# Attention ahead of routed experts, one core: other places for the pieces of the routing tables

## The chip, the core and the metric

One core of a Trainium2 chip runs the whole program. The metric is the device time of one execution in microseconds (us). The engines are TensorE (PE), VectorE (DVE), ScalarE (ACT), GpSimd (POOL) and SyncE (SP), which here only issues transfers.

## The reference, cut

```python
# q, k, v: (8, 8, 1152, 64); w_gate: (512, 8); w1: (8, 512, 1024); w2: (8, 1024, 512)
q_pool = q.reshape(B, H, S // 2, 2, D).mean(axis=3)
scores = q_pool @ k.T / sqrt(D)
attn = softmax(scores)                       # 1152 keys, row maximum subtracted
x = (attn @ v) -> (4608, 512)
logits = x @ w_gate                          # 8 experts, 576 tokens each at most
# tokens go to experts in the order of all logits, the largest first
for e in range(8):
    out[mask_e] = relu(x[mask_e] @ w1[e]) @ w2[e]
```

## The kernel before, in words

The 64 heads are worked on in 32 pairs of two heads. A pair has 18 steps, one for each head and block of 128 keys (`step`). In a step TensorE forms the scores of 576 pooled queries (L751), ScalarE writes their exponentials P in float32 (L754), and a remainder PM is formed, which is P less its upper sixteen bits, in float16 (L758). Of the eighteen remainders of a pair sixteen run on GpSimd and two, in all pairs but the first and the last, on VectorE (steps 4 and 12, `AT["pd"]`). Five steps later TensorE multiplies both parts with the values (L768).

While a pair is in these steps the next one is prepared: QS, KD and VD are loaded; one load of QS, which adds the second of two queries to the first, is issued by GpSimd (L486), once a pair. VectorE forms the low parts QL (L591) and KL in two halves (L610), and those of the values (L645). For an upper bound of the scores TensorE multiplies KH with the queries and VectorE takes maxima from two PSUM banks (L671, L680), gathers them (L703) and, after a transpose on TensorE (L723), writes AU (L724), which a transfer puts into QB. TensorE's next product into bank mb waits for AU.

The second half of the program routes the tokens and runs the experts. It needs constants (a triangle, counting rows, a diagonal, `slots`, `same16` and others), which `routing_tables` makes (L299 to L345): counts with iota first, then fifteen pieces on GpSimd and one on VectorE. They are handed out one to a pair, from the fourth pair on: `table` (L956) raises `od.base` by one with each piece. All of them write the key "tables", so in the planned order each one stands behind the one ahead of it, whichever engine has it.

The order of all work in the attention is set by `Cycle.plan`: an item's key is a number from the table TAU (by its tag, in a cycle of 25) plus 25 times its pair; items are taken by the least key once all that they need has been taken, and each engine's instructions are written in that order. The tag of GpSimd's pieces is "tab", that of VectorE's "tad", that of the remainders "pm". A piece that is planned does not wait for the one ahead on another engine at run time, unless it reads what that wrote.

Of the kernel before, what the change touches and what calls it, by code (L numbers as in the profile page):

```python
# [22 lines left out]
OP = mybir.AluOpType  # L23
# [129 lines left out]
class Cycle(Order):  # L153
# [11 lines left out]
    def plan(self):  # L165
# [45 lines left out]
       12.1143, 0.0557, 20.0132, 22.5039, 25.3261, 28.3165], "ql": [-38.1313], "rc": [9.2364, -9.47], "sc":  # L211
       [-36.4174], "scv": [-30.065], "spr": [-21.9235, -31.1405, -21.9627, -26.5265, -22.5479, -164.2155, -315.3032,
       -74.6622, -15.1485, -17.1123, -19.956, -16.4269], "store": [-95.7261], "sx": [16.3692, 22.2312, 0.8466,
       -61.2066, -78.1894], "tab": [-69.9737], "tad": [-127.8336], "tap": [-44.6145, -41.1498, -47.4908, -31.2065],
       "vh": [-26.7285, -47.8828], "vl": [-23.1603, -21.3115], "vs": [-148.6017, -208.4574], "vsh": [-168.3274],
       "wsq": [12.8365], "x": [-94.3595, -7.6786]}
TAU0 = {"abk": [-60.377, -62.9993], "abs": [-96.8953, -53.0217], "aug": [-7.39949, -0.804], "augt": [-7.399491,
# [58 lines left out]
def routing_tables(nc, pool, ident, jp, scratch, do):  # L276

    J = NBLK
    G = nc.gpsimd

    def one(shape, dt, name):
        return pool.tile(shape, dt, name=name)

    C = dict(ident=ident, before=one([128, 128], BF, "before"), upto=one([128, 128], BF, "upto"),
             ones=one([128, 128], BF, "mones"), e8=one([128, J, E], BF, "e8"), pcol=one([128, 1], F32, "pcol"),
             nib=one([128, 5, 16], F32, "nib"), diag=one([128, 64], F16, "diag"), same16=one([128, 128], F16, "same16"),
             slots=one([128, 640], F16, "slots"), slot1=one([128, 5], F32, "slot1"), jval=one([128, J], F32, "jval"),
             zero=one([128, J], F32, "zero"), TAB=one([128, 2, J + 2], F16, "TAB"), pcol2=one([128, 2], F32, "pcol2"),
             U=one([128, J], F32, "U"), asg=one([128, J], BF, "asg"), CAPS=one([128, E], F32, "CAPS"),
             KC=one([128, 2 * E + 6 + 3 * J], F32, "KC"), ru=one([128, J], BF, "ru"), W=one([128, 40, E], BF, "W"))  # L290
    it = {}
    at = 0
    for name, n in (("e8", J * E), ("p", 1), ("16", 16), ("d", 64), ("m", 128), ("s", 640), ("s1", 5), ("p2", 2)):
        it[name] = scratch[:, at:at + n]
        at += n
    it8 = it["e8"].rearrange("p (j e) -> p j e", e=E)

    def count(dur, ap, pattern, base, step):
        do("POOL", dur, lambda: nc.gpsimd.iota(ap, pattern=pattern, base=base, channel_multiplier=step))  # L299

    count(680, it8, [[0, J], [-1, E]], E, 0)
    count(80, it["p"], [[0, 1]], 0, 1)
    count(80, it["p2"], [[1, 2]], 0, 2)
    count(100, it["16"], [[1, 16]], 1, 0)
    count(210, it["d"], [[-16, 8], [0, 8]], 0, 1)
    count(240, it["m"], [[-1, 128]], 128, 1)
    count(1150, it["s"], [[1, 640]], 0, 0)
    count(90, it["s1"], [[128, 5]], 1, 1)

    def state():  # L310
        nc.gpsimd.memset(C["ones"], 1.0)
        nc.gpsimd.memset(C["zero"], 0.0)
        nc.gpsimd.memset(C["U"], 1.0)
        nc.gpsimd.memset(C["asg"], 0.0)
        nc.gpsimd.memset(C["CAPS"], float(CAP))

        KC = C["KC"]
        nc.gpsimd.memset(KC, 0.0)
        for q in range(5):
            nc.gpsimd.memset(KC[:, 2 * E + q:2 * E + q + 1], 16.0 ** q / 2)  # L320
        nc.gpsimd.memset(KC[:, 2 * E + 6:2 * E + 6 + J], float(CAP))
    do("POOL", 210, state)

    k1 = scratch.bitcast(F32)[:, at:at + 64]
    pieces = [
        (250, lambda: G.tensor_scalar(C["before"], jp, 0.0, None, op0=OP.is_gt)),
        (250, lambda: G.tensor_scalar(C["upto"], jp, 0.0, None, op0=OP.is_ge)),
        (600, lambda: G.tensor_copy(C["e8"], it8)),
        (120, lambda: (G.tensor_copy(C["pcol"], it["p"]), G.tensor_copy(C["pcol2"], it["p2"])))]
    for t in range(4):  # L330
        pieces.append((130, lambda t=t: (G.tensor_scalar(C["nib"][:, t], it["16"], float(16 ** t), None, op0=OP.mult),
                                         G.memset(C["nib"][:, t, 15:16], 3e9))))
    pieces += [
        (70, lambda: G.tensor_scalar(C["nib"][:, 4], it["16"], -1.0, None, op0=OP.add)),
        (250, lambda: (G.tensor_scalar(k1, it["d"], 0.0, None, op0=OP.is_ge),
                       G.tensor_scalar(C["diag"], it["d"], 16.0, None, op0=OP.is_lt))),
        (120, lambda: G.tensor_tensor(C["diag"], C["diag"], k1, op=OP.mult)),
        (1000, lambda: (nc.vector.tensor_scalar(it["m"], it["m"], 15, None, op0=OP.bitwise_and),
                       nc.vector.tensor_scalar(C["same16"], it["m"], 0.0, None, op0=OP.is_equal))),
        (1200, lambda: G.tensor_copy(C["slots"], it["s"])),  # L340
        (160, lambda: (G.tensor_copy(C["slot1"], it["s1"]),
                       G.tensor_scalar(C["jval"], it["s"][:, :J], 128.0, None, op0=OP.mult))),
        (120, lambda: [G.tensor_copy(C["TAB"][:, z, J + 1:J + 2], it["p"]) for z in range(2)]),
        (130, lambda: (G.tensor_copy(C["KC"][:, :E], C["e8"][:, 0]),
                       G.tensor_copy(C["KC"][:, 2 * E + 5:2 * E + 6], C["pcol"])))]  # L345
    for dur, fn in pieces:
        do("DVE" if dur == 1000 else "piece", dur, fn)
    return C


def attention(ctx, tc, top, kt, qt, v, wg, w1, x_dram, L, npair=NPAIR):
# [604 lines left out]
    def table(eng, dur, fn):  # L956
        pools.append(eng == "POOL")
        od.base = max(4, od.base + 1) if eng != "POOL" else 2 + sum(pools) // 4
        od.add(NSTEP * (od.base + 1), "DVE" if eng == "DVE" else "POOL", dur, fn, w=["tables"], lock=True,
               tag={"DVE": "tad", "POOL": "tap", "piece": "tab"}[eng])  # L960
    C = routing_tables(nc, top, ident, jp, scratch, table)
    early += best_early(C)
    if npair > H * NE:
# [687 lines left out]
```

## Time and profile before

| | us |
|---|---|
| three timed runs | 1263.82, 1265.13, 1270.05 |
| their median | 1265.13 |
| the profiled execution | 1275.09 |
| its span, from the first instruction to the last | 1273.3 |
| attention, to the gate's last product, about | 800 |
| granted clock of TensorE, mean | 0.98 |

All views are of the one profiled execution. A row of an engine's order of time has the start, the length, the engine, the line, the operation, what it writes and reads, how many were merged, and in brackets how long the engine had stood idle and what ended that. The length counts from the start of an instruction on its engine, so it holds time in which the instruction is held up there.

### The profile page before, as it was taken

What the parts mean: (1) busy time and instruction counts of PE and PEld (TensorE: products, weight loads), DVE (VectorE), ACT (ScalarE), POOL (GpSimd) and SP (SyncE); (2) the same over time, 40 slices, a digit from 0 to 9 for tenths busy, and PEclk for the clock granted to TensorE, in tenths of its full rate; (3) what the DMA queues carried; (4) which work ended last, traced back from release to release, by engine and by line L of the source; (5) the groups of instructions that cost most, each with busy time, mean ns of one, the idle gap of its engine ahead of it and who ended that gap; (6) DMA issues with size and microseconds to landing.
All of it is one profiled execution on the core that took longest, in us unless ns stands there. A gap on an engine that the chain in (4) does not pass through costs nothing.

```text
span 1273.3 us, 38899 instructions
## 1 busy us (share of the span) xinstructions
PE 1202.7 (94%) x15470; PEld 865.0 (68%) x15470; DVE 1034.3 (81%) x2743; ACT 974.6 (77%) x1719; POOL 905.9 (71%) x879
## 2 busy tenths in 40 slices
PE   7899899898999999999999999789899899999998
PEld 2567677776777777877777778565657466565563
DVE  5889899898999999999999995788878788884520
ACT  6779789797899999999999986076765676767751
POOL 5779799697889988888898897055756474665641
PEclk7999999898999999999999999999999999999999
DMA  6676677566667768677776731043254454537401
GB/s 184 159 187 171 155 174 189 142 163 164 170 162 196 178 163 203 169 171 192 174 187 162 183 91 37 20 170 112 97 195 125 133 172 135 170 124 230 119 30 38
DMA packets 131218, 190.83 MB, mean 150 GB/s; under 512 B 50268, under 2 KB 86108, under 8 KB 128732
## 3 DMA queue, kind: packets, MB, share of 16 engines
q1 hardware_dynamic: 117948, 126.75, 37.9%
q0 software_dynamic: 12944, 61.58, 17.0%
q8 instruction: 121, 1.98, 0.7%
q14 instruction: 61, 0.50, 0.1%
q10 hardware_dynamic: 144, 0.02, 0.0%
HBM read 116.41 MB, written 18.87 MB: 106 GB/s over the span
## 4 chain that ended last, share of the span: by engine, by line
PE 69%; DVE 17%; ACT 4%; issue 3%; DMA 3%; SPq 1%; POOL 1%; another core or an unknown queue 1%; POOLq 0%; ACTq 0%; DVEq 0%
PE sc L751 19%; PE av L768 16%; PE ph L1536 9%; PE po L1566 8%; PE mb L668 5%; PE ma L668 4%; DVE MX L671 2%; DVE KL L610 1%; PE av L803 1%; DMA XG<-XB 1%; DVE PM L758 1%; DVE GE L1163 1%; DVE HX L1545 1%; DMA BD<-QH 1%; PE av L815 1%
## 5 line engine op out<-in xcount | busy, mean ns | idle before, releaser
L758 POOL TENSOR_TENSOR PM<-P 128x576 f16<-128x576 f32 x508 | 618.3, 1277 | 117.2 <-ACT P L754 65.2
L754 ACT ACTIVATE P<-sc,EX 128x576 f32<-128x576 f32 x576 | 412.7, 738 | 97.2 <-PE sc L751 84.2
L768 PEld LDWEIGHTS <-P 128*128 128x128 bf16 x5760 | 297.2, 98 | 31.3 <-issue 2.6
L768 PE MATMUL av<-V,P 128*128 128x65 f16 (+1 forms) x5760 | 305.3, 193 | 0.0
L768 PE MATMUL av<-V,PM 128*128 128x65 f16 x2880 | 296.4, 195 | 0.0
L768 PEld LDWEIGHTS <-PM 128*128 128x128 f16 x2880 | 265.7, 97 | 0.0
L751 PE MATMUL sc<-QA,KA 128*128 128x288 f16 x1152 | 236.7, 287 | 1.6 <-ACT P L754 1.3
L751 PE MATMUL sc<-QB,KB 65*128 65x288 f16 (+1 forms) x1152 | 237.9, 287 | 0.0
L671 DVE TENSOR_REDUCE MX<-mb 128x1 f32<-128x512 f32 x279 | 190.9, 684 | 32.3 <-PE mb L668 27.3
L671 DVE TENSOR_REDUCE MX<-ma 128x1 f32<-128x512 f32 x279 | 191.0, 685 | 13.3 <-PE ma L668 10.1
L751 PEld LDWEIGHTS <-KA 128*128 128x128 f16 x1152 | 106.9, 97 | 86.0 <-issue 34.9
L1566 PE MATMUL po<-W2H,HX 128*128 128x512 f16 x512 | 156.9, 381 | 0.3 <-ACT OT L1568 0.3
L1536 PE MATMUL ph<-XH,W1H 128*128 128x320 f16 (+1 forms) x512 | 146.3, 286 | 0.7 <-DVE WE L1514 0.3
L1536 PE MATMUL ph<-XL,W1H 128*128 128x320 f16 (+1 forms) x512 | 146.2, 286 | 0.8 <-DVE XL L1395 0.3
L1536 PE MATMUL ph<-XH,W1L 128*128 128x320 f16 (+1 forms) x512 | 145.9, 286 | 0.9 <-issue 0.9
L751 PEld LDWEIGHTS <-KB 65*128 65x128 f16 (+1 forms) x1152 | 113.3, 98 | 30.4
L1566 PEld LDWEIGHTS <-HX 128*128 128x128 f16 x768 | 71.6, 98 | 86.4 <-issue 9.6
L1588 POOL DMA_INDIRECT out_dram<-OT,idx x40 | 39.1, 979 | 118.9 <-ACT OT L1568 99.7
L668 PE MATMUL mb<-KH,BD 128*128 128x512 f16 x279 | 107.3, 384 | 13.6 <-DVE AU L724 11.3
L1536 PEld LDWEIGHTS <-W1H 128*128 128x128 f16 x1024 | 97.5, 98 | 33.2 <-issue 7.7
L668 PE MATMUL ma<-KH,BD 128*128 128x512 f16 x279 | 106.8, 383 | 5.9 <-DMA BD<-QH 2.4
L1489 POOL TENSOR_TENSOR W2L<-W,W2H 128x512 f16<-128x512 f32 x64 | 73.3, 1158 | 40.8 <-ACT W L1487 33.6
(308 smaller groups left out, 2169.7 us busy)
## 6 DMA issues: line engine op xcount, KB each, us to landing
KD<-in_kt_dram SPq DMA_DIRECT2D x64, 288.0 KB
VD<-in_v_dram SPq DMA_DIRECT2D x32, 576.0 KB
WB<-in_w_dram SPq DMA_DIRECT2D x32, 512.0 KB
QA<-QH SPq DMA_DIRECT2D x128, 72.0 KB
KA<-KH SPq DMA_DIRECT2D x64, 144.0 KB
KA<-KL SPq DMA_DIRECT2D x64, 144.0 KB
KB<-KH SPq DMA_DIRECT2D x64, 144.0 KB
x_dram<-X SPq DMA_DIRECT2D x16, 576.0 KB
```

The lines of the kernel that those rows point to most:

```text
L610: fn=lambda h=h: nc.vector.scalar_tensor_tensor(KL[n % 2][:, h], KD[n % 2][:, h], KS, KH[i][:, h], op0=OP.mult, op1=OP.subtract),
L668: od.add(t, "PE", 214, lambda: nc.tensor.matmul(m, BD[i][:, j, :], KH[i][:, 512 * c:512 * c + 512], start=True, stop=True), r=bd + [("KH", ...
L671: od.add(t, "DVE", 597, lambda: nc.vector.tensor_reduce(MX[i][:, j, c:c + 1], m, axis=AX.X, op=OP.max), r=[mk], w=[("MX", i, j, c)], tag=" ...
L751: nc.tensor.matmul(c[:, t, :288], a[i][:rows, s, ks], b[i][:rows, s, 288 * t:288 * t + 288], start=first, stop=not first)
L754: od.add(g + 0.1, "ACT", 624, lambda: nc.scalar.activation(p.rearrange("p (t q) -> p t q", t=2), c[:, :, :288], AF.Exp, scale=EX[n % 3][:, ...
L758: od.add(g + 0.2, en, dur, lock=1, fn=lambda: eng.tensor_tensor(pm, p, hi, op=OP.subtract), r=[("P32", g % NP)], w=[("PM", g % NM)], tag="pm")
L768: nc.tensor.matmul(out, w[:, qs], v, start=kb == 0 and j == 0 and y == 0, stop=kb == NKB - 1 and y == 2, skip_group_check=True)
L803: nc.tensor.transpose(m[:, 128 * z:128 * z + 128], X[u][:, 3 * q + z], ident)
L1489: od.add(tt, "POOL", 1230, lambda o=lo[p], a=raw[p], h=hi[p]: nc.gpsimd.tensor_tensor(o, a, h, op=OP.subtract), r=[key, hk, sk], w=[(nm + ...
L1536: nc.tensor.matmul(p, a[:, d, fs], b[:, d, qs], start=z == 0, stop=z == 11)
L1566: nc.tensor.matmul(o, a[:, z, q0:q0 + 128], b[:, z], start=z == 0 and y == 0, stop=z == 7 and y == 2)
L1588: st = nc.gpsimd.indirect_dma_start(out=out, out_offset=bass.IndirectOffsetOnAxis(ap=idx[i][:n, c:c + 1], axis=0), in_=OT[ob][:n], in_offs ...
```

## The change

The key of GpSimd's pieces goes from -69.9737 to -60.4, later by 9.57 in the cycle of 25. VectorE's piece, two operations that were one item, becomes two items. Each item raises the pair by one, so the four pieces behind it (slots, slot1 with jval, TAB, KC) go one pair later as well. No instruction is added or taken away.

```diff
--- before.py
+++ after.py
@@ -211,7 +211,7 @@
        12.1143, 0.0557, 20.0132, 22.5039, 25.3261, 28.3165], "ql": [-38.1313], "rc": [9.2364, -9.47], "sc":
        [-36.4174], "scv": [-30.065], "spr": [-21.9235, -31.1405, -21.9627, -26.5265, -22.5479, -164.2155, -315.3032,
        -74.6622, -15.1485, -17.1123, -19.956, -16.4269], "store": [-95.7261], "sx": [16.3692, 22.2312, 0.8466,
-       -61.2066, -78.1894], "tab": [-69.9737], "tad": [-127.8336], "tap": [-44.6145, -41.1498, -47.4908, -31.2065],
+       -61.2066, -78.1894], "tab": [-60.4], "tad": [-127.8336], "tap": [-44.6145, -41.1498, -47.4908, -31.2065],
        "vh": [-26.7285, -47.8828], "vl": [-23.1603, -21.3115], "vs": [-148.6017, -208.4574], "vsh": [-168.3274],
        "wsq": [12.8365], "x": [-94.3595, -7.6786]}
 TAU0 = {"abk": [-60.377, -62.9993], "abs": [-96.8953, -53.0217], "aug": [-7.39949, -0.804], "augt": [-7.399491,
@@ -335,8 +335,8 @@
         (250, lambda: (G.tensor_scalar(k1, it["d"], 0.0, None, op0=OP.is_ge),
                        G.tensor_scalar(C["diag"], it["d"], 16.0, None, op0=OP.is_lt))),
         (120, lambda: G.tensor_tensor(C["diag"], C["diag"], k1, op=OP.mult)),
-        (1000, lambda: (nc.vector.tensor_scalar(it["m"], it["m"], 15, None, op0=OP.bitwise_and),
-                       nc.vector.tensor_scalar(C["same16"], it["m"], 0.0, None, op0=OP.is_equal))),
+        (1000, lambda: nc.vector.tensor_scalar(it["m"], it["m"], 15, None, op0=OP.bitwise_and)),
+        (1000, lambda: nc.vector.tensor_scalar(C["same16"], it["m"], 0.0, None, op0=OP.is_equal)),
         (1200, lambda: G.tensor_copy(C["slots"], it["s"])),
         (160, lambda: (G.tensor_copy(C["slot1"], it["s1"]),
                        G.tensor_scalar(C["jval"], it["s"][:, :J], 128.0, None, op0=OP.mult))),
```

GpSimd, from the remainder ahead of the piece upto (L327) to behind the next load of QS, before:

```order
L758 TENSOR_TENSOR PM_153<-P_143 128x576
L758 TENSOR_TENSOR PM_156<-P_146 128x576
L327 TENSOR_SCALAR upto<-jp 128x128
L758 TENSOR_TENSOR PM_155<-P_145 128x576
L758 TENSOR_TENSOR PM_157<-P_147 128x576
L758 TENSOR_TENSOR PM_150<-P_140 128x576
L758 TENSOR_TENSOR PM_159<-P_149 128x576
L758 TENSOR_TENSOR PM_152<-P_142 128x576
L758 TENSOR_TENSOR PM_151<-P_141 128x576
L758 TENSOR_TENSOR PM_153<-P_143 128x576
L486 DMA QS_124<-in_qt_dram 128x576
```

The same place in the changed kernel:

```order
L758 TENSOR_TENSOR PM_159<-P_149 128x576
L758 TENSOR_TENSOR PM_152<-P_142 128x576
L758 TENSOR_TENSOR PM_151<-P_141 128x576
L327 TENSOR_SCALAR upto<-jp 128x128
L758 TENSOR_TENSOR PM_153<-P_143 128x576
L486 DMA QS_124<-in_qt_dram 128x576
L758 TENSOR_TENSOR PM_154<-P_144 128x576
```

The piece has moved past six remainders and stands behind all but one of those ahead of the load L486. The other pieces move alike, the first (L326) past two remainders only.

VectorE, both places of its piece (- before, + the changed kernel):

```order
@@ -555,6 +555,4 @@
 L645 SCALAR_TENSOR_TENSOR V_104<-VD_123,SC_114,V_104 128x9x64
 L671 TENSOR_REDUCE MX_139<-mb 128x1
-L338 TENSOR_SCALAR scratch<-scratch 128x128
-L339 TENSOR_SCALAR same_182<-scratch 128x128
 L680 TENSOR_REDUCE MX_139<-ma 128x4
 L671 TENSOR_REDUCE MX_139<-mb 128x1
@@ -577,4 +575,6 @@
 L680 TENSOR_REDUCE MX_139<-mb 128x4
 L671 TENSOR_REDUCE MX_139<-ma 128x1
+L338 TENSOR_SCALAR scratch<-scratch 128x128
+L339 TENSOR_SCALAR same_182<-scratch 128x128
 L591 SCALAR_TENSOR_TENSOR QL_91<-QS_124,SC_115,QH_89 128x576
 L610 SCALAR_TENSOR_TENSOR KL_87<-KD_119,SC_115,KH_85 128x576
```

The two operations (L338, L339) leave the maxima of the value stage and stand directly ahead of QL (L591) and KL (L610).

## Rows read from the trace of the kernel before

**Rows 1.** The page's part 1: busy us, share of the span, instructions.

```profile
PE 1202.7 (94%) x15470; PEld 865.0 (68%) x15470; DVE 1034.3 (81%) x2743; ACT 974.6 (77%) x1719; POOL 905.9 (71%) x879
```

**Rows 2.** Busy times by stretch; PEclk is the granted clock; cut at L724.

```profile
core 0: us, PE busy (x) PEld busy (x) DVE busy (x) ACT busy (x) POOL busy (x), PEclk, DMA share, GB/s
518.56:702.47 183.91, 183.41 (x3050) 145.54 (x3051) 169.58 (x336) 168.91 (x293) 159.07 (x137) 1.00 0.73 179
107.86:158.93 51.07, 47.31 (x762) 37.45 (x761) 46.49 (x85) 42.01 (x74) 40.46 (x37) 0.97 0.62 163
204.98:257.59 52.61, 48.89 (x764) 38.27 (x761) 46.53 (x84) 42.40 (x74) 40.31 (x39) 0.94 0.63 157
281.15:332.98 51.83, 47.90 (x757) 37.28 (x755) 46.60 (x84) 42.37 (x73) 40.63 (x38) 0.93 0.63 159
136.00:140.00 4.00, 4.00 (x54) 3.26 (x51) 2.06 (x4) 3.08 (x5) 1.84 (x2) 0.57 0.54 137
332.98:357.30 24.32, 23.13 (x373) 18.21 (x373) 22.37 (x45) 21.04 (x38) 20.12 (x19) 1.00 0.73 183
```

**Rows 3.** VectorE in order of time, stalled pair: start us, us, what.

```profile
123.89 1.32 DVE L758 TENSOR_TENSOR PM<-P 128x576 f16<-128x576 f32 x1
...
127.79 1.70 DVE L758 TENSOR_TENSOR PM<-P 128x576 f16<-128x576 f32 x1
...
130.43 3.29 DVE L610 SCALAR_TENSOR_TENSOR KL<-KD,SC,KH 128x576 f16<-128x576 f32 x1
...
134.52 0.33 DVE L724 TENSOR_SCALAR AU<-mb,EX 9x128 f16<-9x128 f32 x1
```

**Rows 4.** GpSimd in order of time, the same stretch.

```profile
123.46 2.76 POOL L758 TENSOR_TENSOR PM<-P 128x576 f16<-128x576 f32 x2
127.73 1.15 POOL L758 TENSOR_TENSOR PM<-P 128x576 f16<-128x576 f32 x1 [1.51 <-issue]
128.82 0.88 POOL L486 DMA_DIRECT2D QS<-in_qt_dram  x1
129.47 3.62 POOL L758 TENSOR_TENSOR PM<-P 128x576 f16<-128x576 f32 x3
```

**Rows 5.** TensorE in order of time: two waits, in brackets.

```profile
134.90 0.38 PE L668 MATMUL mb<-KH,BD 128*128 128x512 f16 x1 [3.35 <-DVE AU L724]
343.35 0.38 PE L668 MATMUL ma<-KH,BD 128*128 128x512 f16 x1 [1.08 <-DVE MX L680]
```

**Rows 6.** VectorE in order of time, undisturbed pair.

```profile
375.62 0.81 DVE L591 SCALAR_TENSOR_TENSOR QL<-QS,SC,QH 128x576 f16<-128x576 f32 x1
376.34 0.81 DVE L610 SCALAR_TENSOR_TENSOR KL<-KD,SC,KH 128x576 f16<-128x576 f32 x1
377.07 0.75 DVE L758 TENSOR_TENSOR PM<-P 128x576 f16<-128x576 f32 x1
...
378.75 0.81 DVE L610 SCALAR_TENSOR_TENSOR KL<-KD,SC,KH 128x576 f16<-128x576 f32 x1
```

**Rows 7.** GpSimd in order of time, the same stretch.

```profile
374.29 1.21 POOL L758 TENSOR_TENSOR PM<-P 128x576 f16<-128x576 f32 x1 [0.41 <-ACT P L754]
377.56 1.26 POOL L758 TENSOR_TENSOR PM<-P 128x576 f16<-128x576 f32 x1 [2.06 <-issue]
378.77 0.87 POOL L486 DMA_DIRECT2D QS<-in_qt_dram  x1
```

**Rows 8.** VectorE and GpSimd in order of time, third stall.

```profile
302.18 0.90 POOL L486 DMA_DIRECT2D QS<-in_qt_dram  x1
...
302.49 4.59 DVE L610 SCALAR_TENSOR_TENSOR KL<-KD,SC,KH 128x576 f16<-128x576 f32 x1 [0.25 <-issue]
```

**Rows 9.** GpSimd in order of time: two pieces of the tables.

```profile
118.52 0.54 POOL L327 TENSOR_SCALAR upto<-jp 128x128 bf16<-128x128 int32 x1
...
391.03 0.71 POOL L340 CAST slots<-scratch 128x640 f16<-128x640 int32 x1
```

**Rows 10.** VectorE in order of time: its piece of the tables.

```profile
341.03 0.56 DVE L338 TENSOR_SCALAR scratch<-scratch 128x128 int32<-128x128 int32 x1
341.63 1.07 DVE L339 TENSOR_SCALAR same<-scratch 128x128 f16<-128x128 int32 x1
```

## The prediction

> **What bounds the kernel now.** I read the page first, for the busiest engine [rows 1]: TensorE is busy 94% of the span and nothing else is near it. Then the busy times by stretch, cut where VectorE writes AU (L724), which it does once in each pair of heads [rows 2]. Eight pairs from 518.56 to 702.47 take 183.91 us, 22.99 a pair, with TensorE busy 183.41 of it at a granted clock of 1.00: there TensorE is the bound and GpSimd's lateness costs nothing. The pieces of the tables all lie earlier. There, three stretches of two pairs each take 51.07, 52.61 and 51.83 us where 2 x 22.99 = 45.98 would do, at a mean clock of 0.97, 0.94 and 0.93. They are 5.09, 6.63 and 5.85 us too long, 17.57 together. That is the sum which this change can touch.
>
> Next, VectorE's order of time inside the first such stretch [rows 3]. The second half of KL (L610) starts at 130.43 and takes 3.29 us; one unhindered takes 0.81, as the second L610 row of the undisturbed pair shows [rows 6]. AU stands behind it and comes at 134.52, and TensorE has then waited 3.35 us for it [rows 5]; behind that wait, from 136 to 140, the granted clock is 0.57 [rows 2], near the lower of its two levels (1.2 of 2.4 GHz), and most of the remaining loss lies there. GpSimd's order of time [rows 4] shows what holds KL: a load of QS is issued at 128.82, and behind it three remainders run without a gap from 129.47 to 133.09. KL ends 0.6 us after the last of them.
>
> In an undisturbed pair [rows 6, 7] KL starts at 378.75, together with GpSimd's issue (378.77), and is through before the first remainder behind it. So **KL must start no later than that issue**. What made it late is one step further back. In the stalled pair GpSimd's remainder ahead of the issue starts at 127.73, and VectorE's own remainder at 127.79, 0.06 later; it takes 1.70 instead of 0.75 and ends 0.61 after GpSimd's. In the undisturbed pair VectorE's starts at 377.07, 0.49 before GpSimd's 377.56, and GpSimd waits. VectorE was late there because its earlier remainder, at 123.89, took 1.32 instead of 0.75: GpSimd's run of remainders had not ended yet, two of them taking 2.76 from 123.46. A piece of the tables (upto, 0.54 us at 118.52 [rows 9]) stands in that run.
>
> The stall of the second stretch has the same rows, shifted. The third differs [rows 8]: KL started 0.31 behind the issue at 302.18 after 0.25 us in which the profile shows nothing that it waited for, and took 4.59. A piece is not its visible cause.
>
> **The change part by part.** On GpSimd nothing is added or removed. Each of the fifteen groups moves past two remainders (the first) or six, and most then stand behind the remainder that VectorE's earlier one competes with, ahead of the last remainder before the load of QS. Those from slots on also go one pair later. In that place GpSimd stands idle 2.06 us in the undisturbed pair [rows 7], since its next operand comes from ScalarE. The longest piece, slots, takes 0.71 [rows 9], and the gap covers it. GpSimd's own time there: 0. In the run that they leave, remainders end up to 0.7 us earlier, and VectorE's earlier remainder is free again. For that I take out the two stalls of this kind: 5.09 + 6.63 = 11.72 us in the profiled execution. Bounds: 0, if the lateness has another source, and 17.57 with the third stall. I keep the third, since its late start is not the pieces' doing.
>
> What hides a piece in its new place could fail. QL (L591) starts at 375.62, 0.12 behind the end of the remainder at 374.29 to 375.50 [rows 6, 7]; a piece that starts at once holds it. A held operation ends 0.61 behind GpSimd's, by the remainder of 127.79 [rows 3, 4]. With slots: 375.46 + 0.71 + 0.61 = 376.78 instead of 376.43, so QL is 0.35 late, KL's first half and VectorE's remainder with it: that starts at 377.42, still 0.14 ahead of GpSimd's. upto (0.54) gives 0.18. So no piece alone turns the order over, by this sum.
>
> The two VectorE operations (same16) move past some twenty rows and come directly ahead of QL. In the old place the second takes 1.07 us, the maximum behind it is late, and TensorE waits 1.08 us [rows 5, 10]; that pair takes 24.32, 1.33 more than 22.99 [rows 2]. No row shows both unhindered. Between 0 (they fall into a wait) and the 1.6 us of both, I take 0.5: AU, 128 wide as well, takes 0.33 [rows 3], and such operations overlap by 0.09 with the next, as QL does with KL (0.81 long, 0.72 apart [rows 6]); 2 x 0.24. QL, KL, the remainder and AU queue behind them: 1.33 - 0.5 = 0.8 us won. TensorE's, ScalarE's and SyncE's orders are unchanged; SyncE's copies of QL and KL wait for VectorE as before.
>
> The sum against the profiled execution's 1275.09 us: 1275.09 - 11.72 - 0.8 = 1262.6. The three timed runs have a median of 1265.13, 9.96 below it. They differ among themselves by 6.2 us, about one stall (5.09 to 6.63). I read this as timed runs with one or two stalls rather than three, so that one of the pieces' kind is there to be taken: (5.09 + 6.63) / 2 = 5.9, and 0.8. **1265.13 - 5.9 - 0.8 = 1258.4.**
>
> A page weighs against the size. The rows have KL held through three remainders in one case and until the last of GpSimd's in the other. The Trainium skill, "SBUF — State Buffer", section "Who interferes with whom", says that a VectorE instruction with two SBUF inputs contends with a GpSimd instruction that reads SBUF, and that whoever issues first has the shared pair for the whole instruction. By that KL would be held by one remainder, 1.2 us of the three's 3.62 [rows 4], and two such holds would be worth 2.4 us at the most instead of 11.7. The rows, with 3.29 and 4.59 for one KL, decide, and the sum goes by them.
>
> **The rivals.**
> *A new stall in the new place (slower).* QL is held by a piece or by the two VectorE operations; VectorE's second remainder then starts behind GpSimd's, is held 1.1 us, KL misses the issue and stalls. It decides at a delay of 0.49 us, the distance of 377.07 to 377.56. slots comes to 0.35, the two VectorE operations to 0.5 by my estimate, and diag's two pieces, which stand in a row, may hold it twice. Each new stall costs 5.1 to 6.6. With two more than the median run has: 1265.13 + 11.7 - 0.8 = 1276; with one more 1270.2. For it speaks that the margins are tenths of a microsecond; against it, that undisturbed pairs have all of 0.49 and the largest delays stay below or at it.
>
> *No change.* The stalls that the timed runs hold are of the third kind, or one goes and one comes: 1265.13 - 0.8 = 1264. For it: the third stall has no piece in its rows, and VectorE's instructions ahead of 302 are the same, so it may return. Against it: later pairs without pieces show none in eight.
>
> *Profiling alone makes the 9.96.* Then the timed runs hold all three stalls: 1265.13 - 12.5 = 1252.6, and 1246.7 if the third goes too.
>
> **How the numbers follow.** About 0.5%, 6.3 us, is what a measurement of this kernel can tell from none. Forecast, one stall fewer: 0.40, on both sides of 1258.8. Profiling rival: 0.20. No change: 0.27. Slower: 0.13, of which the upper half lies beyond 1271. Faster by more than 0.5%: 0.20 and a little over half of the forecast's, with part of it reached by a second stall gone, 0.46. Within: 0.43. Slower: 0.11. The range reaches from all three gone, 1247, to one more, 1270.
>
> **What would show it.** Right: in stretches cut at L724 none of the early pairs above 24 us but at most one; KL at 0.8 us throughout; VectorE's first remainder at 0.75 to 0.9; pieces in the gap ahead of the last remainder before L486; 0.5 us or less of TensorE waiting for AU; a granted clock of 1.00 in these pairs. QL longer than 0.81 in pairs with long pieces shows the delay that I price. Wrong: KL of 3 us or more in the pair of slots, diag or same16; VectorE's first remainder still above 1.2; or all gone and the time not moved, so that the timed runs never had the stalls.

## The result, and the profile after

| | before | with the change |
|---|---|---|
| timed runs beside the prediction, us | 1256.53 to 1270.05, median 1264.47 (4 runs) | 1244.15 to 1250.79, median 1247.95 (4 runs) |
| ratio, 95% interval | | 0.9879 (0.9835 to 0.9923) |
| timed again later | 1259.15 to 1272.26, median 1262.39 (11 runs) | 1240.24 to 1246.35, median 1242.79 (6 runs) |
| ratio, 95% interval | | 0.9841 (0.9806 to 0.9877) |
| profiled execution, us | 1275.09 | 1244.15 |
| from the third write of AU to the last | 770.99 - 107.86 = 663.13 | 754.20 - 107.28 = 646.92 |

The kernel is faster by 1.2 to 1.6%. The last row is the attention without its start, and it is the better measure: 16.2 us of gain there, against medians that differ by 16.5 and 19.6.

The same stretches as in [rows 2], of the changed kernel, cut at L724 again; columns as there. The first three are the pairs that held the stalls, the fourth the pair of VectorE's piece, the last the second half of the program:

```profile
core 0: us, PE busy (x) PEld busy (x) DVE busy (x) ACT busy (x) POOL busy (x), PEclk, DMA share, GB/s
107.28:152.99 45.71, 45.71 (x767) 36.26 (x761) 42.24 (x85) 42.28 (x74) 40.73 (x37) 1.00 0.71 180
198.69:244.38 45.69, 45.69 (x767) 36.26 (x761) 42.20 (x84) 42.28 (x74) 40.55 (x39) 1.00 0.73 180
267.54:316.81 49.27, 45.73 (x760) 36.01 (x759) 45.97 (x84) 42.38 (x74) 41.14 (x38) 1.00 0.68 167
316.81:340.16 23.35, 23.33 (x374) 18.25 (x375) 21.39 (x44) 21.48 (x39) 20.44 (x19) 1.00 0.75 190
754.20:1242.40 488.20, 461.90 (x3770) 297.94 (x3764) 343.54 (x1388) 306.24 (x567) 260.40 (x287) 0.99 0.38 123
```

The first two stretches fell from 51.07 and 52.61 us to 45.71 and 45.69, TensorE is busy through all of both, and its granted clock is back at 1.00. The third stretch still holds its stall. The second half of the program, in the kernel before, by the same view:

```profile
770.99:1273.30 502.31, 462.95 (x3770) 295.74 (x3764) 343.96 (x1388) 307.09 (x567) 260.93 (x287) 0.99 0.37 120
```

That half took 14.1 us longer in the profiled execution of the kernel before, with TensorE as busy as after; in the nine other profiles below it takes 485 to 489 (the span less the start of the last AU). No instruction of it was changed.

VectorE in order of time, changed kernel: the pair of upto (answers to [rows 3]), the third stall, and the pair of slots:

```profile
123.69 0.79 DVE L758 TENSOR_TENSOR PM<-P 128x576 f16<-128x576 f32 x1
...
125.60 0.80 DVE L591 SCALAR_TENSOR_TENSOR QL<-QS,SC,QH 128x576 f16<-128x576 f32 x1
...
127.05 0.74 DVE L758 TENSOR_TENSOR PM<-P 128x576 f16<-128x576 f32 x1
...
128.73 0.81 DVE L610 SCALAR_TENSOR_TENSOR KL<-KD,SC,KH 128x576 f16<-128x576 f32 x1
...
288.88 4.59 DVE L610 SCALAR_TENSOR_TENSOR KL<-KD,SC,KH 128x576 f16<-128x576 f32 x1 [0.25 <-issue]
...
404.16 1.16 DVE L591 SCALAR_TENSOR_TENSOR QL<-QS,SC,QH 128x576 f16<-128x576 f32 x1
...
405.98 0.75 DVE L758 TENSOR_TENSOR PM<-P 128x576 f16<-128x576 f32 x1
...
407.66 0.81 DVE L610 SCALAR_TENSOR_TENSOR KL<-KD,SC,KH 128x576 f16<-128x576 f32 x1
```

GpSimd in order of time, the pair of upto and the pair of slots (answers to [rows 4, 7]):

```profile
124.25 1.23 POOL L758 TENSOR_TENSOR PM<-P 128x576 f16<-128x576 f32 x1 [0.40 <-ACT P L754]
125.45 0.54 POOL L327 TENSOR_SCALAR upto<-jp 128x128 bf16<-128x128 int32 x1
127.53 1.27 POOL L758 TENSOR_TENSOR PM<-P 128x576 f16<-128x576 f32 x1 [1.54 <-issue]
128.75 0.88 POOL L486 DMA_DIRECT2D QS<-in_qt_dram  x1
...
404.00 0.71 POOL L340 CAST slots<-scratch 128x640 f16<-128x640 int32 x1
406.10 1.63 POOL L758 TENSOR_TENSOR PM<-P 128x576 f16<-128x576 f32 x1 [1.39 <-issue]
```

In the pair of upto VectorE's first remainder takes 0.79 instead of 1.32, its second starts at 127.05, 0.48 ahead of GpSimd's, and KL goes with the issue (128.73 and 128.75) in 0.81 us. The piece lies in GpSimd's idle time, of which 1.54 us are left. In the pair of slots QL is held, 1.16 us instead of 0.81: 0.35 late, as worked out ahead. VectorE's second remainder (405.98) is still 0.12 ahead of GpSimd's (406.10), and KL is not held. Beside upto QL takes 0.80 (125.60) and is not held at all, where 0.18 had been worked out.

VectorE, then GpSimd, in order of time, VectorE's own piece in its new place:

```profile
335.01 0.22 DVE L338 TENSOR_SCALAR scratch<-scratch 128x128 int32<-128x128 int32 x1
335.27 0.23 DVE L339 TENSOR_SCALAR same<-scratch 128x128 f16<-128x128 int32 x1
335.41 0.81 DVE L591 SCALAR_TENSOR_TENSOR QL<-QS,SC,QH 128x576 f16<-128x576 f32 x1
...
336.87 0.75 DVE L758 TENSOR_TENSOR PM<-P 128x576 f16<-128x576 f32 x1
```

```profile
337.03 1.59 POOL L758 TENSOR_TENSOR PM<-P 128x576 f16<-128x576 f32 x1 [2.16 <-issue]
```

The two operations put QL off by 0.40 us (335.01 to 335.41), and VectorE's remainder stays 0.16 ahead of GpSimd's.

### The profile page after: what moved, and what is told of

It is laid out like the page before. It is cut to its first block, busy times and chain, and to the rows that moved or that the text cites. A ratio compares the mean times of both kernels' runs of the same rounds, so it can differ in the third digit from the quotient of the medians.

```text
span 1242.4 us, 38895 instructions
## 1 busy us (share of the span) xinstructions
PE 1193.8 (96%) x15470; PEld 862.5 (69%) x15470; DVE 1020.9 (82%) x2743; ACT 973.7 (78%) x1719; POOL 901.8 (73%) x879
## 4 chain that ended last, share of the span: by engine, by line
PE 77%; DVE 11%; DMA 5%; ACT 3%; issue 2%; POOL 1%; SPq 0%; POOLq 0%; ACTq 0%; DVEq 0%
PE sc L751 21%; PE av L768 18%; PE ph L1536 11%; PE po L1566 10%; PE mb L668 5%; PE ma L668 5%; DMA W<-in_w_dram,widx 2%; DVE MX L671 2%; PE av L803 1%; ACT P L754 1%; PE av L815 1%; PE rt L1169 1%; DVE HX L1545 1%; DVE GE L1163 1%; PE po L1572 1%
```

## The experiments

The measure is the time from the third write of AU to the last, and the pairs in it whose second half of KL is held for over 3 us. It leaves out the start of the program, where the first AU comes between 53.0 and 59.8 us from one profile to the next. Where I had written down an absolute time of the last AU, that scatter of up to 6.8 us is in it.

| kernel | third to last AU, us | pairs with a held KL of over 3 us | time, us |
|---|---|---|---|
| before | 663.13 | upto, second nib, third stall | 1264.04 (11 runs) |
| the change | 646.92 and 648.68 | third stall | 1242.79 (6 runs) |
| later key alone | 648.58 | third stall | 1244.45 (4 runs) |
| split alone | 670.07 | upto, second nib, third stall, slots | 1266.89 (one) |
| two pieces back | 660.09 | upto, second nib, third stall | 1253.43 (one) |
| slots longer | 654.71 | third stall, slots | 1253.07 (one) |
| change and eight memsets | 642.55 and 641.88 | none | 1236.74 (5 runs) |
| before and eight memsets | 665.82 | upto, second nib, diag | 1263.31 (one) |
| before, QS issued earlier | 675.08 | none | 1277.40 (one) |

A single time says little, since the kernel before alone ranged from 1256.18 to 1272.26; the rows marked (one) are read by their second and third columns.

### The key alone, and the split alone

```diff
 the later key alone, against the kernel before
-  "tab": [-69.9737]
+  "tab": [-60.4]
 the split alone, against the changed kernel
-  "tab": [-60.4]
+  "tab": [-69.9737]
```

> The later key alone, VectorE's piece still one item (so slots and the three pieces behind it stay one pair earlier). Measured by the last write of AU (L724) in the profile: 770.99 us before, 754.20 with the whole change. Theory (the stalls come from pieces in the run of remainders): both stalls of 130 and 227 us gone, last AU at 754 to 756, time within 3 us of the whole change. Rival (the split makes the gain): last AU at 768 or later, time as before.

> The split alone, old key. Theory: KL of about 3.3 us near 130 and 228 us stay, and the third of 4.59 near 302; last AU within 2 us of 771. Rival (the split makes the gain): last AU near 754 to 758, no KL above 1 us but the third.

The key alone gives 648.58 us and no stall but the third; its timed runs have a ratio of 0.9838 (0.9784 to 0.9891) to the kernel before. The last AU came at 760.56, outside what I had expected, because the first came 5.6 us later than with the whole change. The split alone keeps the two stalls and gains nothing. It even brings one: slots, a pair later and in the old place, now stalls its own pair (VectorE's remainder 1.70 us at 423.68, KL 3.27 at 426.31), which I had not expected. So the gain is the key's; the split adds none that can be measured beside it (648.58 against 646.92 and 648.68). VectorE's piece takes its new place with the key alone, too: its pair takes 23.35 us there as well.

### Two pieces put back

```diff
         pools.append(eng == "POOL")
+        old = len(pools) - 1 - sum(pools) in (1, 5)
...
-               tag={"DVE": "tad", "POOL": "tap", "piece": "tab"}[eng])
+               tag={"DVE": "tad", "POOL": "tap", "piece": "tabo" if old else "tab"}[eng])
```

> The whole change, but two of the fifteen pieces, upto (L327) and the second nib (L331), keep their old key and so stand in the middle of the run of remainders of the two pairs that stalled before. Theory (a piece stalls its own pair): KL of 3.3 us in these two pairs, and only there beside the third; each costs 5.4 and 6.9 us with the pair behind it, last AU at 754.2 + 12.3 = 766.5. Rival (lateness gathers over several pairs, or one piece is too short to matter): none or one of the two stalls, last AU at 754 to 761.

VectorE in order of time, the two pairs with a piece in its old place:

```profile
125.93 1.71 DVE L758 TENSOR_TENSOR PM<-P 128x576 f16<-128x576 f32 x1
...
128.57 3.28 DVE L610 SCALAR_TENSOR_TENSOR KL<-KD,SC,KH 128x576 f16<-128x576 f32 x1
...
223.99 1.70 DVE L758 TENSOR_TENSOR PM<-P 128x576 f16<-128x576 f32 x1
...
226.62 3.28 DVE L610 SCALAR_TENSOR_TENSOR KL<-KD,SC,KH 128x576 f16<-128x576 f32 x1
```

GpSimd in order of time, the first of them:

```profile
116.66 0.54 POOL L327 TENSOR_SCALAR upto<-jp 128x128 bf16<-128x128 int32 x1
117.18 7.18 POOL L758 TENSOR_TENSOR PM<-P 128x576 f16<-128x576 f32 x6
125.88 1.15 POOL L758 TENSOR_TENSOR PM<-P 128x576 f16<-128x576 f32 x1 [1.52 <-issue]
```

The two pairs with the pair behind each, by the view of the busy times:

```profile
106.10:158.03 51.93, 48.18 (x761) 37.81 (x759) 46.50 (x84) 42.01 (x74) 40.42 (x37) 0.93 0.64 159
203.73:254.75 51.02, 47.33 (x767) 37.10 (x761) 46.15 (x85) 42.47 (x74) 40.82 (x39) 0.97 0.63 162
```

Both stalls are back, in these two pairs and no others, from pieces of 0.54 and of 0.35 us. They cost 51.93 - 45.71 = 6.2 and 51.02 - 45.69 = 5.3 us, 11.5 together where 12.3 was expected. GpSimd's remainder at 125.88 starts 0.05 ahead of VectorE's 125.93, as in [rows 3, 4]. A piece stalls its own pair; lateness does not gather over several.

Not every piece in the old place does it. VectorE, then GpSimd, in order of time, kernel before: the pair of slots (at 400) and the one behind it, which has pieces too (at 423):

```profile
396.42 1.48 DVE L758 TENSOR_TENSOR PM<-P 128x576 f16<-128x576 f32 x1
...
400.48 0.75 DVE L758 TENSOR_TENSOR PM<-P 128x576 f16<-128x576 f32 x1
...
423.61 0.75 DVE L758 TENSOR_TENSOR PM<-P 128x576 f16<-128x576 f32 x1
```

```profile
400.64 1.59 POOL L758 TENSOR_TENSOR PM<-P 128x576 f16<-128x576 f32 x1 [1.74 <-issue]
...
423.65 1.72 POOL L758 TENSOR_TENSOR PM<-P 128x576 f16<-128x576 f32 x1 [1.61 <-issue]
```

VectorE's first remainder is held longer behind slots (1.48) than behind upto (1.32), yet its second is still 0.16 ahead of GpSimd's, and nothing stalls; in the pair behind it 0.04 is enough. The third stall aside, the order of the two decides in every pair behind the second write of AU, in all ten profiles whose load of QS has its old key: GpSimd's remainder starts 0.05 to 0.43 ahead in the eleven pairs that stall, and VectorE's is level or ahead in all others.

### A longer piece in the new place

```diff
+    long = one([128, 1000], F16, "slots")
-             slots=one([128, 640], F16, "slots"),
+             slots=long[:, 360:],
...
-        (1200, lambda: G.tensor_copy(C["slots"], it["s"])),
+        (1200, lambda: G.tensor_copy(long, scratch[:, 137:1137])),
```

> The whole change with the longest piece made longer: the copy of slots is 1000 columns wide instead of 640 (the 360 ahead of it are read by nothing), so about 1.07 us instead of 0.71. By the sum of the prediction QL is then late by 1.07 + 0.61 + 0.04 less than 0.81 + 0.12 of its own, about 0.7 us, more than the 0.49 by which VectorE's remainder stands ahead of GpSimd's. Theory (order of the two remainders decides): in the pair of slots QL takes about 1.5 us, VectorE's second remainder 1.7, the second half of KL about 3.3, the pair about 27 us; nothing else changes, last AU 5 to 7 us later than with the change. Rival (the delay only shifts the pair): QL 1.5, KL 0.81, the pair 24 us at most.

VectorE, then GpSimd, in order of time, the pair of slots (lines stand one higher here):

```profile
407.46 1.46 DVE L592 SCALAR_TENSOR_TENSOR QL<-QS,SC,QH 128x576 f16<-128x576 f32 x1
...
409.57 1.70 DVE L759 TENSOR_TENSOR PM<-P 128x576 f16<-128x576 f32 x1
...
412.20 3.28 DVE L611 SCALAR_TENSOR_TENSOR KL<-KD,SC,KH 128x576 f16<-128x576 f32 x1
```

```profile
407.29 1.01 POOL L341 CAST slots<-scratch 128x1000 f16<-128x1000 int32 x1
409.38 1.27 POOL L759 TENSOR_TENSOR PM<-P 128x576 f16<-128x576 f32 x1 [1.08 <-issue]
```

With 1.01 instead of 0.71 us QL is 0.65 late, GpSimd's remainder starts 0.19 ahead of VectorE's, and the whole chain of the stall follows; the pair takes 27.14 us. So the order of the two remainders decides, at a delay between 0.35 (no stall) and 0.65; the estimate was 0.49. This is the rival on the slower side, and with the pieces as they are VectorE's remainder stays 0.12 us clear of it.

### Eight memsets, with the change and without

```diff
     nc.vector.memset(floor[:, 3:], 512.0 * PEAK)
+    tick = const.tile([1, 8], F32, name="tick")
+    for i in range(8):
+        nc.vector.memset(tick[:, i:i + 1], 0.0)
```

> The whole change and eight VectorE memsets of one column at the start of the program, some 0.5 us in all, whose result nothing reads. The third stall stands at the same place of VectorE's instruction stream in both kernels, behind 0.25 us that wait for nothing shown. Theory A (that gap belongs to a place in the instruction stream): the KL that took 4.59 us near 289 us takes 0.81, the pair of 26.73 us takes about 23, last AU some 3 us earlier, at 751, time 3 us less than with the change. Theory B (the gap belongs to the work at that point): KL is 4.59 again in the same pair, last AU at 754 to 755.

VectorE, then GpSimd, in order of time, the pair of the third stall (lines three higher):

```profile
286.13 0.82 DVE L613 SCALAR_TENSOR_TENSOR KL<-KD,SC,KH 128x576 f16<-128x576 f32 x1
```

```profile
286.13 0.89 POOL L489 DMA_DIRECT2D QS<-in_qt_dram  x1
```

Eight more instructions far ahead take away the 0.25 us gap and with it the third stall: KL starts with the issue and takes 0.82. So the gap goes with the place in VectorE's instruction stream (theory A) rather than with the work that stands there: all eight profiles without the memsets have it ahead of this KL, the three with them do not. What happens at that place no run here shows; nor that the shift of the instructions does it alone, since the memsets also bring a small tile of their own. The time was 1238.10 us (1236.18 to 1242.44), 0.9807 of the kernel before (0.9765 to 0.9848). I ran it once more beside the change alone, on one chip:

> The whole change once more, on the chip of the next run, to set the two side by side. Theory (the order of instructions fixes the stalls, so every execution of a kernel has the same ones): the third stall is there again, KL 4.59 us near 289, third to last AU within 3 us of 646.9; the time 1.2 to 1.6% under the kernel before. Rival (stalls come and go with the execution): another set of pairs above 25 us.

> The change with the eight memsets once more, beside it. Theory: no pair above 25 us from the third on, third to last AU within 3 us of 642.6, the time 4 to 6 us under the change alone. Rival: the 4.4 us of the first profile do not return, the two times within 2 us of each other.

The change alone took 1240.24 to 1246.35 us, with the memsets 1235.80 to 1238.66: the ranges don't meet, the medians differ by 6.1 us, and third to last AU by 6.8 (648.68 and 641.88). This is the fastest version here, 0.9788 (0.9753 to 0.9824) of the kernel before. In the change's second profile the third stall is back, in the same pair and again 4.59 us long, and no other: in these two profiles the stall comes with the kernel, not with the execution.

> The kernel before with the eight VectorE memsets at the start. Theory (three stalls of two kinds, independent of each other): KL of 3.3 us stays in the pairs of upto and of the second nib, the KL of 4.59 takes 0.81; the time between the third and the last AU is 663 less 5 to 6 us. Rival (the memsets shift the whole program against something else, and that is what removed the third stall): other pairs stall, or none does.

In the kernel before, the memsets remove the third stall too (KL 0.82 at 304.66), and the two others stay. Yet nothing was won, 665.82 against 663.13: the pair behind it, which held no KL as long as the third stall stood ahead of it, now stalls by itself. VectorE in order of time, then GpSimd (lines three higher):

```profile
326.95 1.70 DVE L761 TENSOR_TENSOR PM<-P 128x576 f16<-128x576 f32 x1
...
329.58 3.29 DVE L613 SCALAR_TENSOR_TENSOR KL<-KD,SC,KH 128x576 f16<-128x576 f32 x1
```

```profile
326.52 1.52 POOL L761 TENSOR_TENSOR PM<-P 128x576 f16<-128x576 f32 x1 [1.14 <-issue]
```

It is the pair of diag, whose pieces stand in the run of remainders. So the stalls are not independent of each other, and only half of what I had expected came: with the pieces in the old place, taking one stall away brought another.

### The load of QS issued one remainder earlier

```diff
 against the kernel before
-  "qa": [-57.085]
+  "qa": [-58.5]
```

> The kernel before, pieces in their old places, but in each pair GpSimd issues the load of QS (L486) one remainder earlier, in its idle time ahead of the last remainder instead of behind it. Theory A (what holds KL for three remainders is the queue that runs without a gap behind an issue): no KL above 2.0 us in any pair, VectorE's remainders still held in the same pairs (1.0 to 1.7 us), the two pairs of 26.7 us down to 23 to 24.5. Theory B (any run of remainders holds KL so): KL of 3 us or more in many pairs, since now a remainder follows directly behind the one ahead of KL; time above the kernel before.

VectorE, then GpSimd, in order of time, the pair of upto:

```profile
133.74 1.72 DVE L758 TENSOR_TENSOR PM<-P 128x576 f16<-128x576 f32 x1
...
136.39 1.79 DVE L610 SCALAR_TENSOR_TENSOR KL<-KD,SC,KH 128x576 f16<-128x576 f32 x1
```

```profile
132.12 0.88 POOL L486 DMA_DIRECT2D QS<-in_qt_dram  x1
133.70 5.48 POOL L758 TENSOR_TENSOR PM<-P 128x576 f16<-128x576 f32 x4 [0.70 <-issue]
```

GpSimd runs four remainders without a pause here, and KL, 2.7 us into the run, is held for one of them only: 1.79 us, in no pair more than 1.80. VectorE's remainder at 133.74, 0.04 behind the first of the run, is held for one as well (1.72). So it is the run directly behind an issue that holds KL to its end, theory A. The third stall is gone here too, though its gap is not:

```profile
306.25 1.46 DVE L610 SCALAR_TENSOR_TENSOR KL<-KD,SC,KH 128x576 f16<-128x576 f32 x1 [0.25 <-issue]
```

The same 0.25 us stand ahead of the same KL, but the issue (302.55) is 3.7 us past by then, and KL takes 1.46 us instead of 4.59.

As a remedy it fails: KL is now held by one remainder in most pairs, also in those that never stalled, and the attention takes 675.08 us, more than with three stalls; the pairs of 26.7 came down to 25.0 and 26.5 only, less than I had expected.

The Trainium skill, "SBUF — State Buffer", section "Who interferes with whom", has the loser held for the whole instruction of the other engine. These rows agree with that: one remainder, 1.79 instead of 0.81. Behind an issue they don't: 3.28 for the same operation, three instructions of GpSimd long.

## Why the prediction was right, and where not

- *Which stalls go.* Right, and the cause is shown: the two of the pieces' kind went, the third stayed with 4.59 us and its 0.25 us gap. Two pieces put back bring back exactly these two.
- *What they cost.* The two were put at 5.09 + 6.63 = 11.72 us. The same stretches are shorter by 5.36 + 6.92 = 12.28.
- *QL behind a piece.* Behind slots 0.35 us late was worked out, 0.35 measured, and a piece of 1.01 us tips the order. Behind upto 0.18 was worked out and no delay measured.
- *VectorE's piece.* 0.8 us was worked out; the pair went from 24.32 to 23.35, 0.97. The two operations were put at 0.5 and take 0.40.
- *The sum for the timed runs.* This is the step that failed. I wrote of the 9.96 us between the profiled execution and the median: "I read this as timed runs with one or two stalls rather than three, so that one of the pieces' kind is there to be taken", and took 5.9 where 11.7 stood in the rows. No profile here bears that reading out: both profiles of the change hold the same third stall in the same pair, and each variant with the pieces of upto and of the second nib in the old place and the issue unmoved holds those two. What was slow in that one execution is its second half, 502.31 us against 485 to 489 in all others, which is more than the 9.96. With both stalls the same sum gives 1265.13 - 12.5 = 1252.6, the case that I had priced as a rival and given a chance of 0.20; 1247.95 and 1242.79 were measured. Within the attention the sum of 12.5 compares with 16.2 and 14.4 in the two profiles of the change (663.13 less 646.92 and 648.68). The rest of the first is mostly the pair behind the third stall, 22.54 us there and 25.41 in the second profile, against 25.10 before.
- *That rival's reason, and the range.* Profiling as the source of the 9.96 us is not shown: the profiled executions of the change (1244.15, 1242.42) lie within its timed runs. A gain of 6.7 us was forecast, 16.5 and 19.6 came. That 1247.95 lies within the range, by 0.95 us, is luck: its lower end was priced with the third stall gone, which stayed, and the 1242.79 of the second comparison lies below it.
- *No change and slower* did not come. The slower rival's mechanism is real, as the longer piece shows, but it takes a delay above the 0.35 us of slots; 0.65 was enough.

The last 3 to 5 us between the attention's gain and the medians of the second comparison (16.2 or 14.4 against 19.6) are open, as is what makes the second half differ by 14 us between executions.

## What to carry to other kernels

An engine that has idle time can still be late at one point, and a delay of a few tenths of a microsecond there can turn over who comes first at something shared and cost ten times as much; read who starts first, and by how much, in a good and in a bad pair. When work has to go in anywhere, put it where the engine waits for its next operand, and check the margin to what follows. And before an effect is scaled down because a profile is slower than the timed runs, find the stretch in which the profile is slower.

## What was not expected of the hardware

KL, a VectorE operation with two SBUF operands, that starts 0.31 or 1.6 us behind GpSimd's issue of a transfer waits until GpSimd's run behind the issue ends (4.59 and 3.3 us), while in a run that doesn't stand directly behind an issue it waits for one instruction (1.79 us). And eight instructions of no effect, some 280 us ahead, changed the time by 6.1 us: with them the gap of 0.25 us ahead of the one operation that had to be on time is gone.
